# Gated mix of linear attention and PEER: the sum of the key features taken as one product of ones with a prepared tile

## The chip, the cores and the metric

The kernel runs on one core of a Trainium2 chip. The metric is the device time of one execution in microseconds, from start to end. PE stands for the matrix engine, PEld for its weight loads, DVE, ACT and POOL for the vector, scalar and GpSimd engines, SP for the engine that only issues DMAs.

## The reference

The input x has 2048 rows of 512 values. Two branches read it and a gate mixes them. Branch B is a PEER layer with 32 heads and one expert per head: scores of two halves of a query, the best of 16 in each, a row of u and v chosen by the pair. Branch A is linear attention with 32 heads of 16 and softmax features:

```python
phi_q = concat([softmax(pq), softmax(-pq)]); phi_k = concat([softmax(pk), softmax(-pk)])
kv = einsum("bhsf,bhsd->bhfd", phi_k, v)
z  = einsum("bhsf->bhf", phi_k)          # the sum over all 2048 rows
num = einsum("bhqf,bhfd->bhqd", phi_q, kv)
den = einsum("bhqf,bhf->bhq", phi_q, z)[..., None] + 1e-6
return g * (num / den) @ wo + (1 - g) * b
```

The change concerns z: 32 heads times 32 features, 1024 sums over all rows. Since every row of x needs all of kv and z, the key features of all rows come ahead of the first use of either.

## The kernel before

The rows are worked in 16 tiles of 128, numbered 0 to 15. Single-precision products are split in two parts, a high one and the rest (names ending in h and l, type fp32r), and one logical product is three matmuls: lines L56, L57 and L58 of a helper. The order of every engine's instructions is the order of the Python text; nothing reorders it. An engine takes its list in order, and waits where an operand or a buffer isn't ready.

Stage A (until about 127 us) makes for each tile the key logits `pk`, the features `phis[t]` (tile `d`, 128 rows by 1024: ACT's exponential, then in `ksoft` a DVE sum L200, a DVE reciprocal L201, and POOL's product L202 that normalises), and the values `vs[t]` with a 17th column of ones per head. `kvacc(t)` (L209) is 32 small products, two records each, that add phi_k^T v into one PSUM bank `acc`; the 17th column of that bank collects z, but only for tiles 0 to 13, since the values of tiles 14 and 15 are made later, without the column. For those two, `kvz(t)` (L217) multiplies the features by a column `ones` into the same 17th column, 32 products again. At the end of stage A `fold_q` (L148) folds the feature weights into the query weights, in two halves of PE work; between and after these stand the scores `s` of tile 0 (`front_s(0, 0)`, `front_s(0, 1)`). ACT (wah, L153) and DVE (wal, L154) then split the folded weights.

Between the stages, after `kvz(14)`, come for tile 0: `best` (DVE L475 and L476: maximum and mask of a score), the transposing DMA of that mask to `et` (SP, L482), `front_q` (PE: `pq`), `soft_in` (DVE L94, L96, L98, L100: differences to maximum and minimum, into a new tile `d`), `front_p` (PE: `pp`), then `kvz(15)`. ACT copies z out of the bank into `zc` (128 partitions by 8), `z_final` spreads it over all partitions with eight products of a broadcast column of zc and the identity, in plain fp32 (L663), and ACT copies the outcome to `zb` (128 by 1024, L665).

Stage B goes over the tiles a = 0 to 14 in a loop, and each pass also begins tile a + 1. DVE's gate reciprocal (L390) releases ACT's L398, L399 and L400 (`gelu_act`), behind which stand on ACT's list the two exponentials L426 (`soft_exp`). DVE sums them (L436), POOL multiplies them with zb (L432, `soft_w`), and DVE goes on to the denominators and to `best` and `soft_in` of the next tile. On PE a pass holds `mk` (the mask's product with `et`), `s` of the next tile in two halves, `pp` and `pq`. In pass 1 alone the values of tiles 14 and 15 are made (`pv`, ACT copy L189) and `kvacc(14)` and `kvacc(15)` close the bank, which ACT copies out in `kv_final` (`kvb`, L657). On ACT's list those four copies stand behind L586, which waits for POOL's `cf` (L581); on POOL's list L581 stands behind L432, L755 and L404. PE's `oT` (L518) is the first to use kvb. The bank pools of PSUM have four buffers (`mm`) and three (`tr`).

Of the kernel before, what the change touches and what calls it, by code (L numbers as in the profile page):

```python
# [9 lines left out]
F32 = mybir.dt.float32  # L10
F32R = mybir.dt.float32r
# [5 lines left out]
ALU = mybir.AluOpType  # L17
# [3 lines left out]
P = 128  # L21
# [5 lines left out]
F = 16  # L27
# [8 lines left out]
def mix_kernel(ctx, tc, xT, wqT, wkT, wv, wphi, wo, wq, kk, ug, ev, cst, out):  # L36
# [6 lines left out]
    def mm_bank(name):  # L43
        return psum.tile([P, 512], F32, tag="mm", bufs=4, name=name)
# [32 lines left out]
    kp = per.tile([P, 2, 2, 32], F32, name="kp")  # L77
    sa.append(per.tile([P, 4, 24], U16, name="sa1"))
    sb = [per.tile([P, 4, 24], U16, name=f"sb{i}") for i in range(2)]
    ones = per.tile([P, 1], F32, name="ones")  # L80
    zc = per.tile([P, 8], F32, name="zc")
    per.tile([P, 96], F32, name="rest")

# [56 lines left out]
    def fold_q(raw, wh, wl):  # L140
        o = four("foldq")
        for i in range(2):
            for k in (2 * i, 2 * i + 1):
                for b in range(NK):
                    for q in range(4):
                        r = slice(32 * q, 32 * q + 32)
                        c0 = (k * NK + b) * 32
                        pe.matmul(o[q][:, c0:c0 + 32], raw[r, b, k * P:(k + 1) * P], wp[r, b, :],  # L148
                                  start=True, stop=True, skip_group_check=True)
            yield  # L150
        for q in range(4):
            part = o[q].rearrange("p (g c) -> p g c", c=32)
            act.copy(fv(wh, q), part)  # L153
            dve.tensor_tensor(fv(wl, q), part, fv(wh, q), op=ALU.subtract)  # L154
        yield
# [42 lines left out]
    def ksoft(t):  # L198
        d, st = phis[t], stk.pop(t)
        dve.tensor_reduce(st[:, 64:128], g64(d), axis=AX.X, op=ALU.add)  # L200
        dve.reciprocal(st[:, 128:192], st[:, 64:128])  # L201
        pool.tensor_tensor(g64(d), g64(d), b64(st[:, 128:192]), op=ALU.mult)  # L202

    def kvacc(t):
        n = F + 1 if t < NT - 2 else F
        for g in range(8):
            for c in range(4):
                h = 4 * g + c
                pe.matmul(acc[32 * c:32 * c + 32, g, :n], phis[t][:, 32 * h:32 * h + 32],  # L209
                          vs[t][:, h, :n], start=(t == 0 and g == 0),  # L210
                          stop=(t == NT - 1), skip_group_check=True)

    def kvz(t):
        for g in range(8):
            for c in range(4):
                h = 4 * g + c
                pe.matmul(acc[32 * c:32 * c + 32, g, F:], phis[t][:, 32 * h:32 * h + 32],  # L217
                          ones, start=False, stop=False, skip_group_check=True)

    def score_w(i, raw):  # L220
        j, par = i // 2, i % 2
        if par == 0:
# [48 lines left out]
    for a in sa + sb:  # L271
        pool.memset(a, 0)
    pool.memset(kvb, 0.0)
    pool.memset(ones, 1.0)
    for k in (0, 2, 1, 3):
        if k == 0:
            x_split(0, slice(0, 1))
# [26 lines left out]
    for t in range(NT):  # L304
        if t + 3 < NT:
            x_load(t + 3)
        if 2 < t < NT - 2:
            vproj(t)()
        kproj(t)
        old = [] if t == NT - 3 else list(joins)  # L310
        if old:
            joins.clear()
        for _ in range(plan.get(t, 0)):
            score_w(done, raws[done])
            done += 1
            if done + 1 < 16:
                raws.append(stage(wq[done + 1], f"wq{done + 1}"))
            elif done == 15:
                rawq = stage(wqT, "rawq")
            if done % 2 == 0:  # L320
                score_planes(done // 2 - 1)
        if t == 11:
            rawu = [spare(ug[:, 0:2], "rawu0", [P, 2, NU])]
        if t == 12:
            rawu.append(spare(ug[:, 2:4], "rawu1", [P, 2, NU]))
        if t == 13:
            rawe = [spare(ev[:, 0], "rawe0", [P, D])]
        if t % 2 == 0:
            for u in (t - 3, t - 2):
                if u >= 0:  # L330
                    kvacc(u)
        if 0 < t < NT - 2:
            x_split(t + 2)
        if t == NT - 2:
            score_join(*old.pop())
        elif t == NT - 1:
            for k in range(2):
                split(eh[:, k, :], el[:, k, :], rawe[k])
            fq = fold_q(rawq, wah, wal)
            next(fq)  # L340
            front_s(0, 0)
            next(fq)
            front_s(0, 1)
            kvacc(NT - 3)
            next(fq)
        act.activation(phis[t], phis[t], AF.Exp)  # L346
        if t == NT - 2:
            score_join(*joins.pop())
        if t == 13:
            for k in range(NK):  # L350
                split(uh[:, k, :NU], ul[:, k, :NU], rawu[k // 2][:, k % 2, :])
            rawe.append(spare(ev[:, 1], "rawe1", [P, D]))
        ksoft(t)
        for j, tp in old:
            score_join(j, tp)
    ca.close()
    w2 = ctx.enter_context(tc_pool("w2", "left"))
    zb = w2.tile([P, 1024], F32, name="zb", bufs=1)
    chains = {}

    def step(t, n=1):
# [44 lines left out]
    def front_q(t):  # L406
        pq = mm_bank(f"pq{t}")
        proj(pq, t, wah, wal, 0, D)
        st8[t]["pq"] = pq
# [246 lines left out]
            r = slice(32 * c, 32 * c + 32)  # L656
            act.copy(kvb[r, :, F * (c % 2):F * (c % 2) + F], acc[r, :, :F])  # L657

    def z_final():
        for j in range(2):  # L660
            o = mm_bank(f"z{j}")
            for g in range(4):
                pe.matmul(o[:, g * P:(g + 1) * P], zc[:, 4 * j + g:4 * j + g + 1].to_broadcast([P, P]), ident,  # L663
                          start=True, stop=True)
            act.copy(zb[:, 512 * j:512 * j + 512], o)  # L665

    def wo_load(ks):
        for k in ks:
# [1 line left out]
            sp.dma_start(rawo[k], wo[:, k, :])  # L670

    rawo = {}
    kvz(NT - 2)
    best(0, 0)
    best(0, 1)
    cb.close()
    w3 = ctx.enter_context(tc_pool("w3", "left"))
    turn_eq(0)
    front_q(0)
    soft_in(0)  # L680
    front_p(0, False)
    kvz(NT - 1)
    act.copy(zc, acc[:, :, F])
    gelu_pre(0)
    z_final()
    wo_load((0, 1))
    def dealt(a, b, z):
        def first():
            for _ in gate(a):
                step(b)  # L690
            step(b, 4)
            if z >= 0:
                back_cl(z)

        moves = iter((first, lambda: step(b, 5), lambda: step(b, 2), lambda: None))
        return lambda: next(moves)()

    for a in range(NT - 1):
        n, b, z = a + 1, a - 1, a - 2
        owed = min(18, 3 * max(0, a - DEFER))  # L700
        left = min(18, 3 * max(0, a - DEFER + 1))
        B, Z = b >= 0, z >= 0
        if Z:
            mid_num(z)
        if B:
            planes(b, 0)
            if Z:
                c_join(z)
            planes(b, 1)
            front_q(a)  # L710
        if owed:
            back(z - 1, owed)
            store(z - 1)
        if a == 1:
            v14, v15 = vproj(NT - 2), vproj(NT - 1)
        gelu_in(a)
        if Z:
            num_lo(z)
        if B:
            soft_in(a, dealt(a, b, z))  # L720
            drain(b)
        else:
            for _ in gate(a):
                pass
        gelu_act(a)
        if a == 1:
            v14()
        soft_exp(a)
        if a == 1:
            v15()  # L730
            for k in range(2):
                act.copy(wbh[:, k, :], rawo[k])
        if Z and not left:
            back(z)
            store(z)
        if not left:
            mid_mask(a)
        front_s(n, 0)
        if left:
            mid_mask(a)  # L740
            if left < 18:
                back(z, 18 - left)
        if a == 1:
            kvacc(NT - 2)
            kvacc(NT - 1)
            cl_.close()
            w4 = ctx.enter_context(tc_pool("w4", "right"))
        front_s(n, 1)
        front_p(n, False)
        soft_w(a)  # L750
        soft_sum(a, 0)
        soft_sum(a, 1)
        if a == 1:
            for k in range(2):
                pool.tensor_tensor(wbl[:, k, :], rawo[k], wbh[:, k, :], op=ALU.subtract)  # L755
            wo_load((2, 3))
        best(n, 0)
        soft_y(a, 0)
        soft_y(a, 1)
        soft_p(a)  # L760
        if B:
            join(b)
            gelu_out(b)
            coef(b)
            c_planes(b)
        if a == 1:
            kv_final()
            for k in range(2, NK):
                act.copy(wbh[:, k, :], rawo[k])
        soft_b(a)  # L770
        if a == 1:
            for k in range(2, NK):
                pool.tensor_tensor(wbl[:, k, :], rawo[k], wbh[:, k, :], op=ALU.subtract)
        best(n, 1)
        turn_eq(n)
        gelu_pre(n)
    a, b, z = NT - 1, NT - 2, NT - 3
    neg = w2.tile([P, P], F32R, name="neg", bufs=1)

    def low(lo, o, hi):  # L780
        pe.matmul(o, neg, hi, start=False, stop=True, skip_group_check=True)
# [118 lines left out]
```

## Time and profile before

| what | value |
|---|---|
| time, three runs | 379.95, 380.48 and 380.8 us, median 380.48 us |
| span of the profiled execution (first to last instruction) | 378.1 us |
| that execution's clock | PE granted full speed in all 40 slices |
| PE busy | 372.5 us, 99% of the span |
| DVE, ACT, POOL busy | 315.9, 235.5 and 154.9 us |
| DMA | 46.69 MB, mean 123 GB/s |

The profiled execution has its span of 378.1 us as its own time; the runs were timed from start to end of the program, so that 2.4 us of a median run lie outside of the span. A row of the timeline begins with its start and its duration in us; an instruction's record overlaps with that of the next one on the same engine, so that the price of one in a row of equals is the distance from start to start. "x64" says that neighbouring instructions of one form are joined in a row. In brackets stands how long the engine had nothing to do before, and what ended that.

### The profile page before, as it was taken

Reading aid. Unit: us, or ns where it says so; the run is one execution under the profiler, and the core shown is the slowest. Engines: PE = TensorE matmul, PEld = TensorE weight load, DVE = VectorE, ACT = ScalarE, POOL = GpSimd, SP = SyncE. Lnnn points to the kernel's source line nnn. Section 1 sums busy time; section 2 is a strip of 40 time slices with the busy share of each in tenths; the row PEclk is TensorE's granted clock in tenths of the full one; section 3 lists DMA queues with packets and bytes.
Section 4 is the critical chain, followed back from the end, with each engine's and each line's share of the span. In section 5 each row is a group of like instructions: output and inputs, shape, how many; then the busy total and the mean of one; then the engine's idle time right before and its main releaser. Section 6 shows DMA issues by size and latency. Waiting matters only on the chain.

```text
span 378.1 us, 9073 instructions
## 1 busy us (share of the span) xinstructions
PE 372.5 (99%) x3613; PEld 294.3 (78%) x3613; DVE 315.9 (84%) x776; ACT 235.5 (62%) x420; POOL 154.9 (41%) x164
## 2 busy tenths in 40 slices
PE   8999999999999999999999999999999999999996
PEld 4766777777768888888878888888888888888775
DVE  4479866866868968879999999999999999999993
ACT  4436554644646345769668777696686686687741
POOL 1014435325325232946427335344454454364700
PEclk9999999999999999999999999999999999999999
DMA  7757878478592034242351452441532524523201
GB/s 272 307 187 259 258 218 237 157 222 237 188 305 84 3 85 83 73 83 76 80 99 49 105 84 57 85 100 32 121 62 65 127 56 72 126 52 77 64 34 57
DMA packets 72219, 46.69 MB, mean 123 GB/s; under 512 B 63600, under 2 KB 64496, under 8 KB 69872
## 3 DMA queue, kind: packets, MB, share of 16 engines
q1 hardware_dynamic: 71312, 45.24, 44.6%
q10 hardware_dynamic: 864, 0.87, 0.8%
q8 instruction: 28, 0.46, 0.5%
q14 instruction: 15, 0.12, 0.1%
HBM read 26.43 MB, written 4.19 MB: 81 GB/s over the span
## 4 chain that ended last, share of the span: by engine, by line
PE 97%; DMA 1%; ACT 0%; SPq 0%; DVE 0%; issue 0%; ACTq 0%; DVEq 0%
PE po L627 11%; PE s L56 8%; PE s L57 8%; PE s L58 8%; PE po L634 5%; PE pq L56 5%; PE pv L56 4%; PE pk L56 4%; PE ws L225 4%; PE pv L57 4%; PE pq L58 4%; PE pk L57 4%; PE pq L57 4%; PE pk L58 4%; PE pv L58 4%; PE oT L518 3%
## 5 line engine op out<-in xcount | busy, mean ns | idle before, releaser
L432 POOL TENSOR_TENSOR w<-d,zb 128x512 f32<-128x512 f32 x32 | 40.9, 1294 | 83.4 <-ACT d L426 81.1
L202 POOL TENSOR_TENSOR d<-d,st 128x1024 f32<-128x1024 f32 x16 | 31.0, 1935 | 74.4 <-DVE st L201 40.5
L56 PE MATMUL s<-sh,xh 128*128 128x512 f32 x128 | 51.0, 399 | 0.0
L57 PE MATMUL s<-sl,xh 128*128 128x512 f32 x128 | 49.9, 390 | 0.0
L58 PE MATMUL s<-sh,xl 128*128 128x512 f32 x128 | 49.8, 389 | 0.0
L426 ACT ACTIVATE d<-d 128x512 f32<-128x512 f32 x32 | 20.1, 632 | 38.0 <-DVE d L98 29.3
L467 POOL TENSOR_TENSOR d<-d,st 128x512 f32<-128x512 f32 x30 | 31.2, 1062 | 28.5 <-DVE st L461 25.6
L509 ACT COPY pt<-tp 128x1024 uint16<-128x1024 uint16 x28 | 36.4, 1369 | 1.0 <-PE kvacc L209 1.0
L346 ACT ACTIVATE d<-d 128x1024 f32<-128x1024 f32 x16 | 17.0, 1064 | 28.5 <-DVE d L100 28.5
L499 ACT COPY pl<-d 128x1024 uint16<-128x1024 uint16 x28 | 29.2, 1045 | 4.4 <-POOL d L467 4.4
L58 PEld LDWEIGHTS s<-sh,xl 128*128 128x128 f32 x128 | 24.0, 188 | 5.1
L56 PEld LDWEIGHTS s<-sh,xh 128*128 128x128 f32 x128 | 24.0, 188 | 4.7
L57 PEld LDWEIGHTS s<-sl,xh 128*128 128x128 f32 x128 | 24.1, 188 | 4.5
L56 PE MATMUL pq<-wah,xh 128*128 128x512 f32 x64 | 26.7, 418 | 0.0
L56 PE MATMUL pv<-wbh,xh 128*128 128x512 f32 x64 | 26.0, 407 | 0.0
L436 DVE TENSOR_REDUCE st<-d 128x32 f32<-128x512 f32 x32 | 21.7, 683 | 5.0 <-ACT d L426 3.5
L57 PE MATMUL pv<-wbl,xh 128*128 128x512 f32 x64 | 25.2, 394 | 0.3 <-DVE wbl L51 0.3
L200 DVE TENSOR_REDUCE st<-d 128x64 f32<-128x1024 f32 x16 | 19.5, 1218 | 7.0 <-ACT d L346 7.0
L56 PE MATMUL pk<-wah,xh 128*128 128x512 f32 x64 | 25.3, 396 | 0.0
L58 PE MATMUL pv<-wbh,xl 128*128 128x512 f32 x64 | 25.1, 392 | 0.0
L58 PE MATMUL pq<-wah,xl 128*128 128x512 f32 x64 | 25.1, 392 | 0.0
L57 PE MATMUL pk<-wal,xh 128*128 128x512 f32 x64 | 25.0, 391 | 0.0
(177 smaller groups left out, 1029.5 us busy)
## 6 DMA issues: line engine op xcount, KB each, us to landing
wq<-wq SPq DMA_DIRECT2D x16, 1024.0 KB, 6.0
xr<-xT SPq DMA_DIRECT2D x15, 256.0 KB, 6.0
y<-ot SPq DMA_DIRECT2D x15, 256.0 KB, 2.3
rawk<-wkT SPq DMA_DIRECT2D x1, 1024.0 KB, 6.1
rawq<-wqT SPq DMA_DIRECT2D x1, 1024.0 KB, 5.7
rawo<-wo SPq DMA_DIRECT2D x4, 256.0 KB, 3.8
rawu<-ug SPq DMA_DIRECT2D x2, 258.0 KB, 6.3
rawv<-wv ACTq DMA_DIRECT2D x2, 256.0 KB, 4.2
```

The costliest lines, as they stand in the source:

```text
L56: pe.matmul(o, ah, bh, start=(first and i == 0), stop=False)
L57: pe.matmul(o, ah, bl, start=False, stop=False)
L58: pe.matmul(o, al, bh, start=False, stop=(last and i == n - 1))
L200: dve.tensor_reduce(st[:, 64:128], g64(d), axis=AX.X, op=ALU.add)
L202: pool.tensor_tensor(g64(d), g64(d), b64(st[:, 128:192]), op=ALU.mult)
L426: act.activation(hs(d, i), hs(d, i), AF.Exp)
L432: pool.tensor_tensor(hs(e["w"], i), hs(e["ph"], i), hs(zb, i), op=ALU.mult)
L436: dve.tensor_reduce(pair(e["st"][:, 64:128])[:, :, i], hs(e["ph"], i), axis=AX.X, op=ALU.add)
L467: eng.tensor_tensor(g64(d)[:, gs_], g64(d)[:, gs_], r[:, gs_].unsqueeze(2).to_broadcast([P, 32, F]), op=ALU.mult)
L499: act.copy(pl, e["ph"][:, halves[i]].bitcast(U16).rearrange("p (c j) -> p j c", j=2))
L509: act.copy(p16[:, :, 4 * i:4 * i + 4, :], e["tp"][i].rearrange("p (j g) n -> p j g n", j=2))
L627: pe.matmul(po, a, b, start=(i == 0), stop=False)
```

## The change

z is no longer gathered in the bank to its end. The 17th column is read after tile 13, which therefore has to come first: `kvacc(13)` moves on PE from behind the scores of tile 0 to the place between the first half of `fold_q` and those scores, and ACT's copy to `zc` from behind `kvz(15)` to ahead of the four casts L153. A tile `zsum` (128 by 1024) is made: POOL writes the identity times zc, 128 columns for each of 8 groups (the diagonal), and adds the features of tile 14; both stand on POOL's list ahead of the normalising product of tile 15, behind a memset that fills `neg` with ones (a tile that is filled anew with minus the identity at the program's end, as before). DVE adds the features of tile 15 in two halves, ACT casts each half to its high part, DVE makes the rest. Four matmuls of fp32r, ones by the high part and ones by the rest for each half, sum over the partitions and leave z in every partition. Both `kvz` and the eight fp32 products go. `front_s(1, 0)`, the first half of the next tile's scores, moves ahead of these four matmuls and of `mk`.

The list of SP is unchanged: each transposing DMA and each load stands where it stood. The diff, cut to its core:

```diff
-    def kvz(t):
-        for g in range(8):
-            for c in range(4):
-                h = 4 * g + c
-                pe.matmul(acc[32 * c:32 * c + 32, g, F:], phis[t][:, 32 * h:32 * h + 32],
-                          ones, start=False, stop=False, skip_group_check=True)
...
         elif t == NT - 1:
+            fq = fold_q(rawq, wah, wal)
+            next(fq)
+            kvacc(NT - 3)
             for k in range(2):
                 split(eh[:, k, :], el[:, k, :], rawe[k])
-            fq = fold_q(rawq, wah, wal)
-            next(fq)
+            act.copy(zc, acc[:, :, F])
             front_s(0, 0)
             next(fq)
             front_s(0, 1)
-            kvacc(NT - 3)
             next(fq)
...
-        ksoft(t)
+        if t < NT - 1:
+            ksoft(t)
...
+    neg = w2.tile([P, P], F32R, name="neg", bufs=1)
+    pool.memset(neg.bitcast(F32), 1.0)
+    zsum = w2.tile([P, 1024], F32, tag="w", bufs=1, name="zsum")
+    pool.tensor_tensor(zsum.rearrange("p (g n) -> p g n", n=P), ident.unsqueeze(1).to_broadcast([P, 8, P]),
+                       zc.unsqueeze(2).to_broadcast([P, 8, P]), op=ALU.mult)
+    pool.tensor_tensor(zsum, zsum, phis[NT - 2], op=ALU.add)
+    ksoft(NT - 1)
...
-    def z_final():
-        for j in range(2):
-            o = mm_bank(f"z{j}")
-            for g in range(4):
-                pe.matmul(o[:, g * P:(g + 1) * P], zc[:, 4 * j + g:4 * j + g + 1].to_broadcast([P, P]), ident,
-                          start=True, stop=True)
-            act.copy(zb[:, 512 * j:512 * j + 512], o)
+    def z_parts(z):
+        out = []
+        for i, s_ in enumerate(halves):
+            zh = w3.tile([P, 512], F32R, tag="pl", name=f"zh{i}")
+            zl = w3.tile([P, 512], F32R, tag="tp", name=f"zl{i}")
+            dve.tensor_tensor(z[:, s_], z[:, s_], phis[NT - 1][:, s_], op=ALU.add)
+            act.copy(zh, z[:, s_])
+            out.append((zh, zl))
+        for (zh, zl), s_ in zip(out, halves):
+            dve.tensor_tensor(zl, z[:, s_], zh, op=ALU.subtract)
+        return out
+
+    def z_final(parts):
+        for (zh, zl), s_ in zip(parts, halves):
+            o = tr_bank("z")
+            pe.matmul(o, neg, zh, start=True, stop=False)
+            pe.matmul(o, neg, zl, start=False, stop=True)
+            act.copy(zb[:, s_], o)
...
-    kvz(NT - 2)
     best(0, 0)
     best(0, 1)
...
     front_q(0)
+    zparts = z_parts(zsum)
     soft_in(0)
     front_p(0, False)
-    kvz(NT - 1)
-    act.copy(zc, acc[:, :, F])
     gelu_pre(0)
-    z_final()
+    front_s(1, 0)
+    z_final(zparts)
     wo_load((0, 1))
...
-        front_s(n, 0)
+        if a:
+            front_s(n, 0)
```

Three places of the engines' lists show it. The new text has other line numbers: behind the new lines all of stage B stands one line later up to 644 or so (L94 stays, L475 becomes L476, L432 becomes L433). First PE, from the end of tile 0's `pp` to the first of `mk`, before:

```order
L58 MATMUL pp_1667<-uh,xl 128x258
L217 MATMUL kvacc<-ones,d_1450 32x1 x32
L663 MATMUL z_1721<-cs,zc 128x128 x4
L663 MATMUL z_1727<-cs,zc 128x128 x4
L537 LDWEIGHTS et_1646
```

and after, from the last of the twelve matmuls of `s` of tile 1, first half, which follow `pp`:

```order
L58 MATMUL s_1_1671<-sh,xl 128x512
L675 MATMUL z<-zh_1634,neg 128x512
L676 MATMUL z<-zl_1635,neg 128x512
L675 MATMUL z<-zh_1638,neg 128x512
L676 MATMUL z<-zl_1639,neg 128x512
L538 LDWEIGHTS et_1619
```

The two kinds of plain fp32 products are gone, four matmuls of fp32r stand there, and the scores of tile 1 stand ahead of them. Second DVE, from the mask of tile 0's second half to the sums of pass 0, before:

```order
L476 TENSOR_TENSOR eq_1635<-s_0_1541,mx_0_1639 128x512
L94 TENSOR_REDUCE st_1662<-pq_1648 128x32
L96 TENSOR_REDUCE st_1662<-pq_1648 128x32
L98 TENSOR_TENSOR d_1661<-pq_1648,st_1662 128x32x16
L100 TENSOR_TENSOR d_1661<-st_1662,pq_1648 128x32x16
L390 RECIPROCAL gs_1713<-gs_1713 128x1
L436 TENSOR_REDUCE st_1662<-d_1661 128x32 x2
```

and after:

```order
L477 TENSOR_TENSOR eq_1608<-s_0_1573,mx_0_1612 128x512
L665 TENSOR_TENSOR zsum<-zsum,d_1449 128x512 x2
L669 TENSOR_TENSOR zl_1635<-zsum,zh_1634 128x512
L669 TENSOR_TENSOR zl_1639<-zsum,zh_1638 128x512
L94 TENSOR_REDUCE st_1645<-pq_1621 128x32
L96 TENSOR_REDUCE st_1645<-pq_1621 128x32
L98 TENSOR_TENSOR d_1644<-pq_1621,st_1645 128x32x16
L100 TENSOR_TENSOR d_1644<-st_1645,pq_1621 128x32x16
L391 RECIPROCAL gs_1663<-gs_1663 128x1
L437 TENSOR_REDUCE st_1645<-d_1644 128x32 x2
```

Four instructions of 128 by 512 stand ahead of all of `soft_in`, and so of the reciprocal for which ACT waits. Third POOL, from the normalising product of tile 14 to pass 0's product with zb, before:

```order
L202 TENSOR_TENSOR d_1347<-d_1347,st_1348 128x1024
L202 TENSOR_TENSOR d_1450<-d_1450,st_1451 128x1024
L394 TENSOR_TENSOR x_1717<-x_1717,px_1716 128x256
L432 TENSOR_TENSOR w_1792<-d_1661,zb 128x32x16 x2
L467 TENSOR_TENSOR d_1661<-d_1661,st_1662 128x512 x2
```

and after:

```order
L202 TENSOR_TENSOR d_1346<-d_1346,st_1347 128x1024
L354 MEMSET neg 128x128
L356 TENSOR_TENSOR zsum<-cs,zc 128x1024
L358 TENSOR_TENSOR zsum<-zsum,d_1346 128x1024
L202 TENSOR_TENSOR d_1449<-d_1449,st_1450 128x1024
L395 TENSOR_TENSOR x_1667<-x_1667,px_1666 128x256
L433 TENSOR_TENSOR w_1738<-d_1644,zb 128x32x16 x2
```

Three instructions stand between the normalising products of tiles 14 and 15. By the program's semaphores the memset waits for DVE's first `el` (L51, whose input lay in the same memory), and the product L356 for ACT's zc and for the last matmul of `fold_q`.

More of the change, by code (lines that the diff above doesn't have):

```diff
@@ L79, in mix_kernel @@
     sb = [per.tile([P, 4, 24], U16, name=f"sb{i}") for i in range(2)]
-    ones = per.tile([P, 1], F32, name="ones")
+    per.tile([P, 1], F32, name="ones")
     zc = per.tile([P, 8], F32, name="zc")
@@ L273, in mix_kernel @@
     pool.memset(kvb, 0.0)
-    pool.memset(ones, 1.0)
     for k in (0, 2, 1, 3):
@@ L777, in mix_kernel @@
     a, b, z = NT - 1, NT - 2, NT - 3
-    neg = w2.tile([P, P], F32R, name="neg", bufs=1)
     def low(lo, o, hi):
```

## The prediction

> **What bounds the kernel now.** I read the page's busy shares and chain first, then the busy time by stretches, then the timeline of each engine from 118 to 161 us, where all changed instructions lie but for two short ones at the start.
>
> ```profile
> PE 372.5 (99%) x3613; PEld 294.3 (78%) x3613; DVE 315.9 (84%) x776; ACT 235.5 (62%) x420; POOL 154.9 (41%) x164
> ...
> PE 97%; DMA 1%; ACT 0%; SPq 0%; DVE 0%; issue 0%; ACTq 0%; DVEq 0%
> ```
>
> PE is the bound of the whole, and the chain of waits runs on it to 97%. So PE time that goes is gained, as long as no other engine then arrives later than PE. The stretches (us, then busy time and count for PE, PEld, DVE, ACT and POOL, granted clock) say how near the others are around the change:
>
> ```profile
> 130.00:135.00 5.00, 4.72 (x96) 4.36 (x95) 3.94 (x8) 1.94 (x7) 1.55 (x2) 1.00 0.35 64
> 135.00:145.00 10.00, 10.00 (x59) 8.56 (x59) 6.64 (x19) 4.96 (x12) 4.82 (x6) 1.00 0.17 49
> 145.00:160.00 15.00, 15.00 (x229) 12.13 (x227) 13.74 (x37) 10.19 (x20) 8.60 (x10) 1.00 0.39 95
> ```
>
> Only at 130 to 135 does PE idle at all, 0.28 us. DVE has some 3.4 us to spare at 135 to 145 and hardly any, 1.3 us, at 145 to 160. What DVE gets to do there decides.
>
> **PE: what goes and what comes.** PE's timeline:
>
> ```profile
> 126.52 0.71 PE L209 MATMUL kvacc<-v,d 128*32 128x17 f32 x62
> ...
> 127.09 0.71 PE L217 MATMUL kvacc<-ones,d 128*32 128x1 f32 x62
> 127.74 0.50 PE L56 MATMUL pq<-wah,xh 128*128 128x512 f32 x1
> ...
> 132.16 0.71 PE L217 MATMUL kvacc<-ones,d 128*32 128x1 f32 x64
> 133.15 2.05 PE L663 MATMUL z<-cs,zc 128*128 128x128 f32 x16 [0.28 <-ACT zc L683]
> 135.04 0.35 PE L537 MATMUL mk<-wm,et 128*128 128x16 bf16 x8
> ...
> 135.79 0.39 PE L58 MATMUL s<-sh,xl 128*128 128x512 f32 x1
> ...
> 140.56 0.39 PE L58 MATMUL s<-sh,xl 128*128 128x512 f32 x1
> ...
> 153.54 1.27 PE L209 MATMUL kvacc<-v,d 128*32 128x16 f32 x128
> 154.74 0.50 PE L56 MATMUL s<-sh,xh 128*128 128x512 f32 x1
> ```
>
> - `kvacc(13)` and `kvz(14)` take 127.74 - 126.52 = 1.22 us together, 0.61 each. `kvz(14)` goes: -0.61. `kvacc(13)` only moves; what stands between its new place and its old one comes 0.61 later, the second half of `fold_q` among it.
> - `kvz(15)`, the wait for zc and the eight fp32 products go: from 132.16 to 135.04, -2.88.
> - A 512-column matmul of fp32r costs (140.56 - 135.79) / 21 = 0.227 us. Four come: +0.91. `front_s(1, 0)` costs the same wherever it stands.
>
> PE's own sum is -0.61 - 2.88 + 0.91 = -2.6 us. If that were all, the time would be 377.9 us.
>
> **DVE and ACT: what comes and who waits.** DVE's timeline, then ACT's:
>
> ```profile
> 122.53 2.28 DVE L51 TENSOR_TENSOR el<-rawe,eh 128x512 fp32r<-128x512 f32 x2
> 124.73 2.47 DVE L154 TENSOR_TENSOR wal<-foldq,wah 128x512 fp32r<-128x512 f32 x4
> ...
> 130.82 0.69 DVE L476 TENSOR_TENSOR eq<-s,mx 128x512 bf16<-128x512 f32 x1
> 131.43 0.68 DVE L94 TENSOR_REDUCE st<-pq 128x32 f32<-128x512 f32 x1
> ...
> 133.82 0.16 DVE L390 RECIPROCAL gs<-gs 128x1 f32<-128x1 f32 x1
> ...
> 137.42 1.28 DVE L436 TENSOR_REDUCE st<-d 128x32 f32<-128x512 f32 x2 [3.45 <-ACT d L426]
> ...
> 143.44 0.69 DVE L476 TENSOR_TENSOR eq<-s,mx 128x512 bf16<-128x512 f32 x1
> 145.18 0.69 DVE L94 TENSOR_REDUCE st<-pq 128x32 f32<-128x512 f32 x1 [1.05 <-PE pq L58]
> ...
> 149.75 0.68 DVE L98 TENSOR_TENSOR d<-pq,st 128x512 f32<-128x512 f32 x1
> ```
>
> ```profile
> 123.67 2.06 ACT L153 CAST wah<-foldq 128x512 fp32r<-128x512 f32 x4 [2.22 <-PE foldq L148]
> ...
> 132.94 0.17 ACT L683 COPY zc<-kvacc 128x8 f32<-128x8 f32 x1 [6.26 <-PE kvacc L217]
> ...
> 135.72 0.20 ACT L398 ACTIVATE gs<-gs 128x1 f32<-128x1 f32 x1
> ...
> 136.77 1.14 ACT L426 ACTIVATE d<-d 128x512 f32<-128x512 f32 x2
> ...
> 150.47 0.63 ACT L426 ACTIVATE d<-d 128x512 f32<-128x512 f32 x1 [1.99 <-DVE d L98]
> ...
> 152.26 0.57 ACT L189 COPY v<-pv 128x512 f32<-128x512 f32 x1
> ...
> 157.81 0.62 ACT L586 COPY plc<-cf 128x512 uint16<-128x512 uint16 x1 [0.34 <-POOL cf L581]
> 158.34 1.07 ACT L657 COPY kvb<-kvacc 32x128 f32<-32x128 f32 x4
> ```
>
> - ACT's casts wah wait for `fold_q` and so start at 123.67 + 0.61 with the copy zc (at most 0.17) ahead of them: 124.4. One takes 2.06 / 4 = 0.5, so DVE's first wal can start at 125.0 in place of 124.73. DVE's list is 0.3 late from there on.
> - Four new DVE instructions, two SBUF inputs of 128 by 512 each. Their nearest rows are wal, 2.47 / 4 = 0.62, and the undisturbed el, 0.68 (row below): 2.5 to 2.7, I take 2.58. They start at 131.73. The two casts to zh (0.5 like wah) lie beside the second add and the first subtraction, and ACT has nothing else then (6.26 us idle ahead of 132.94). So `soft_in(0)` starts at 131.43 + 0.3 + 2.58 = 134.31.
> - L390 follows 133.82 - 131.43 = 2.39 later, at 136.70, ending at 136.86. ACT's L398, at 135.72 before, waits for it: +1.15. ACT's copies of zb, which held L398 up before, start behind z at about 134.9 and are over by 136.1; that wait covers them. Behind L398 stand both L426, for which DVE's L436 waits: 138.57. Of DVE's 3.45 us of waiting, 1.75 are left.
> - From L436 to the mask of tile 1's second half DVE hardly stops, so that mask ends at 143.44 + 0.69 + 1.15 = 145.28. Before, DVE then waited 1.05 us for PE's `pq`, until 145.18. Now `pq` has long been there, and L94 of tile 1 starts at 145.28: **+0.1 against before**. 2.88 us of delay have used up 1.70 + 1.05 of waiting.
>
> From there the chain no longer passes PE. The rows of POOL and of the weight loads of `oT`:
>
> ```profile
> 1.58 0.32 POOL L273 MEMSET kvb<- 128x256 f32 x1
> ...
> 121.73 1.93 POOL L202 TENSOR_TENSOR d<-d,st 128x1024 f32<-128x1024 f32 x1
> 129.09 1.94 POOL L202 TENSOR_TENSOR d<-d,st 128x1024 f32<-128x1024 f32 x1 [5.43 <-DVE st L201]
> ...
> 151.18 2.55 POOL L432 TENSOR_TENSOR w<-d,zb 128x512 f32<-128x512 f32 x2 [5.48 <-ACT d L426]
> 153.69 2.56 POOL L755 TENSOR_TENSOR wbl<-rawo,wbh 128x512 fp32r<-128x512 f32 x2
> ...
> 157.04 0.74 POOL L581 TENSOR_TENSOR cf<-cf,px 128x256 f32<-128x256 f32 x1
> ```
>
> ```profile
> 159.46 0.40 PEld L518 LDWEIGHTS oT<-pt,kvb 64*32 64x32 f32 x30 [0.16 <-ACT kvb L657]
> ```
>
> L98 of tile 1 releases L426 (150.47), that releases POOL's L432 (151.18), behind it without a pause come L755 and L581, that releases ACT's L586 (157.81), behind it stand the kvb copies, and PE's `oT` waits for them already, 0.16 us. All of it moves by +0.1. PE arrives with its lead, loses a part at `kvacc(15)` (the copy of v, from 152.26, ends at 152.93; the next `s` starts 0.6 later, at 153.5 against 154.74, a lead of 1.2) and the rest at `oT`. After that, PE-bound as before.
>
> **POOL.** The memset: 128 by 128, under 0.32. The diagonal product has broadcast inputs, like L202: 1.93; with two full inputs, like L755, it would be 2.56. The addition has two full inputs: 2.56. Start at about 124.5 (the end of `fold_q`, 0.61 later than 123.67; and zc). The pair ends at 129.0 to 129.6, where L202 of tile 15 started at 129.09 before, now 129.4 by DVE's 0.3. L202 then ends at 131.3 to 131.6, before DVE's first addition, at 131.73: cost nothing, with 0.1 to 0.4 us left of cover. The two memsets, `ones` gone and `neg` come, lie at no edge. SP's issues keep their order; the transposed mask is due 0.3 later, and `mk` comes after z.
>
> **The sum.** Span 378.1 + 0.1 = 378.2. The median run lay 2.4 us above the span: 380.6 us. Bounds of this case: DVE's four at 2.5 with no shift of wal, -0.3; at 2.7 with POOL 0.2 late, +0.3. That is 380.2 to 381.0.
>
> **Rivals.**
>
> *Faster: DVE's delay is absorbed.* DVE waits 3.45 + 1.05 = 4.5 us between 133.8 and 145.2, more than the 2.88 that come. If L436 weren't tied to L390 through ACT's list, L94 of tile 1 could start 1.05 earlier, the kvb chain would follow, and the time would be 379.4 us. Against it: L398 stands ahead of L426, and its operand comes from L390. The full 377.9 needs kvb off the path as well, against the 0.16 us that `oT` waits already. 0.12 and 0.08.
>
> *Slower: POOL's pair makes tile 15's features late.* DVE's first addition waits for L202 of tile 15, and all above hangs on it 1 to 1. The point is a pair of 5.0 us: 124.5 + 5.0 = 129.5, with 1.94 and a handover 131.5 to 131.7. Each microsecond more costs one. The diagonal product, with both inputs broadcast and in stretches of 128, has no row of its own; at 1 us above its upper bound, 3.6, the time is 381.7 us. Against: POOL's rows go by size, and broadcasting made them shorter, not longer. 0.14.
>
> *Slower: DVE and POOL collide.* The view by line of L51 (count, then shortest, median and longest in ns):
>
> ```profile
> L51 DVE TENSOR_TENSOR el<-rawe,eh x2: 680/1180/1681, 122.5 to 124.1; 128x512 fp32r<-128x512 f32 x2
> ```
>
> The first el took 1.68 us, under POOL's L202 (121.73 to 123.66), the second 0.68. If POOL's diagonal product gets ahead of the second el, that one waits up to 1.93 to 2.56 us, wal, both masks and all of `soft_in` with it: 380.6 + 2 = 382.6 us. The point: the product would have to start before the second el, at 124.1. Against: it waits for `fold_q`, 124.3, and stands behind a memset that waits for the first el. 0.09.
>
> The Trainium skill, page "SBUF — State Buffer", section "Who interferes with whom", states that a DVE instruction with two SBUF inputs and a GpSimd instruction that reads SBUF exclude each other, whoever comes first for its whole length. The two el agree with it, 1.68 against 0.68. By this rule the order at 124.1 to 124.3 decides between this rival and the forecast, 382.6 or 380.6 us; and the four new DVE instructions, of the same kind, cost 0.62 only while POOL stands still, as it does between L202 of tile 15 and the next pass.
>
> **How the numbers follow.** No change (what a measurement of this kernel can tell is about 0.2%, 0.76 us): 0.54, with rounding the rest of 0.57 split to both sides. Faster 0.12 + 0.08 and a bit, 0.21; slower 0.14 + 0.09 and a bit, 0.25. The range leaves out the full gain (0.08) and the collision (0.09): 379.3 to 382.0. The likeliest case alone spans 380.2 to 381.0.
>
> **What would show it.** Right: `mk` of tile 0 about where it was, but `s` of tile 1's second half over 2 us earlier; DVE's wait before L436 down to 1.5 to 2 us and the one before `soft_in(1)` gone; PE waiting some 1.4 us at `kvacc(15)` for v and some 1 us at `oT` for kvb; the kvb copies at 158.4. Wrong: L94 of tile 1 before 144.6 or after 146.0; `oT` not waiting; POOL's pair over 5.0 us; the second el over 0.7.

## The result, and the profile after

The changed kernel takes 380.82 us (median of 14 runs, 380.68 to 381.18), the kernel before in the same comparison 380.53 us. The ratio is 1.0006 with a 95% interval of 0.9997 to 1.0016, from 0.1 us faster to 0.6 us slower: no difference that can be told. The forecast was 380.6 us, between 379.3 and 382.0, no change as the likeliest.

PE's saving is in the profile. Its busy time on the page went from 372.5 to 370.8 us, in a span of 379.0 us. From the page of the changed kernel, the busy shares and the chain that ended last:

```profile
PE 370.8 (98%) x3473; PEld 292.3 (77%) x3473; DVE 319.8 (84%) x780; ACT 236.2 (62%) x422; POOL 159.0 (42%) x166
...
PE 87%; DVE 6%; DMA 1%; ACT 1%; POOL 1%; issue 1%; SPq 0%; ACTq 0%; DVEq 0%
```

The chain ran on PE to 97% before. Now 8% of it runs on DVE, ACT and POOL. PE's three longest waits (line, releaser, us in total, times, longest):

```profile
PE kvacc L209 <- ACT v L189: 1.7, 1, 1.7
PE warm L263 <- POOL tab L246: 1.2, 1, 1.2
PE oT L519 <- ACT kvb L658: 0.8, 1, 0.8
```

The wait at `warm` was there before. The two others are new, 2.42 us together, nearly all of what PE had saved. PE's timeline:

```profile
117.03 1.99 PE L148 MATMUL foldq<-wp,rawq 32*128 32x32 f32 x64
118.94 0.74 PE L209 MATMUL kvacc<-v,d 128*32 128x17 f32 x64
...
134.57 0.40 PE L675 MATMUL z<-zh,neg 128*128 128x512 f32 x1
...
135.51 0.36 PE L538 MATMUL mk<-wm,et 128*128 128x16 bf16 x8
135.72 0.47 PE L56 MATMUL s<-sh,xh 128*128 128x512 f32 x1
...
153.86 0.73 PE L209 MATMUL kvacc<-v,d 128*32 128x16 f32 x64 [1.66 <-ACT v L189]
...
159.76 1.21 PE L519 MATMUL oT<-pt,kvb 64*32 64x128 f32 x32 [0.76 <-ACT kvb L658]
```

The same places before the change, `fold_q`, the second half of tile 1's scores and `oT`:

```profile
116.80 1.99 PE L148 MATMUL foldq<-wp,rawq 32*128 32x32 f32 x64
...
138.06 0.39 PE L56 MATMUL s<-sh,xh 128*128 128x512 f32 x1
...
159.16 0.96 PE L518 MATMUL oT<-pt,kvb 64*32 64x128 f32 x32
```

The second half of tile 1's scores starts at 135.72, against 138.06 before: the lead is there. It is spent at 153.86 and 159.76, and inside of `oT`, which takes 1.21 us in place of 0.96 because its later parts wait for the later copies of kvb. DVE in between:

```profile
131.95 1.28 DVE L665 TENSOR_TENSOR zsum<-zsum,d 128x512 f32<-128x512 f32 x2
133.31 1.30 DVE L669 TENSOR_TENSOR zl<-zsum,zh 128x512 fp32r<-128x512 f32 x2
134.53 0.68 DVE L94 TENSOR_REDUCE st<-pq 128x32 f32<-128x512 f32 x1
...
138.81 1.28 DVE L437 TENSOR_REDUCE st<-d 128x32 f32<-128x512 f32 x2 [1.74 <-ACT d L427]
...
145.44 0.68 DVE L94 TENSOR_REDUCE st<-pq 128x32 f32<-128x512 f32 x1
146.04 0.15 DVE L391 RECIPROCAL gs<-gs 128x1 f32<-128x1 f32 x1
146.11 0.28 DVE L554 TENSOR_TENSOR m<-sa 128x64 uint16<-128x64 uint16 x1
146.31 0.72 DVE L556 TENSOR_TENSOR m<-sa 128x32 uint16<-128x32 uint16 x1
147.07 0.42 DVE L564 TENSOR_TENSOR X<-m,m 128x256 uint32<-128x256 uint32 x1
...
150.64 0.68 DVE L98 TENSOR_TENSOR d<-pq,st 128x512 f32<-128x512 f32 x1
```

The four new instructions take 134.53 - 131.95 = 2.58 us, and the 3.45 us of waiting before the sums of pass 0 shrank to 1.74. ACT's rows show the tie: the copies of zb are over at 136.31, and then L399 waits for DVE's reciprocal.

```profile
135.24 1.07 ACT L677 COPY zb<-z 128x512 f32<-128x512 f32 x2
137.11 0.20 ACT L399 ACTIVATE gs<-gs 128x1 f32<-128x1 f32 x1 [0.80 <-DVE gs L391]
```

Up to L94 of tile 1 all stands as worked out. Then one small instruction, L556, takes 0.72 us, where the same (L555) took 0.17 before. POOL's timeline says what stood there:

```profile
124.85 2.09 POOL L356 TENSOR_TENSOR zsum<-cs,zc 128x1024 f32<-128x1024 f32 x1
127.02 2.41 POOL L358 TENSOR_TENSOR zsum<-zsum,d 128x1024 f32<-128x1024 f32 x1
129.58 1.94 POOL L202 TENSOR_TENSOR d<-d,st 128x1024 f32<-128x1024 f32 x1 [0.16 <-DVE st L201]
...
144.23 2.08 POOL L468 TENSOR_TENSOR d<-d,st 128x512 f32<-128x512 f32 x2 [2.78 <-issue]
146.26 0.74 POOL L395 TENSOR_TENSOR x<-x,px 128x256 f32<-128x256 f32 x1
```

POOL's product x of tile 1 runs from 146.26 to 147.00, and L556 ends then, at 147.03. Before, the same product was over at 145.70, ahead of both mask instructions, as the rows of POOL and DVE before show:

```profile
144.96 0.74 POOL L394 TENSOR_TENSOR x<-x,px 128x256 f32<-128x256 f32 x1
```

```profile
145.98 0.17 DVE L555 TENSOR_TENSOR m<-sa 128x32 uint16<-128x32 uint16 x1
```

In the eleven traces of this document the first half of `fold_q` starts between 116.80 and 117.55 us, and ahead of it the change takes out one memset and nothing else. So traces are compared below by the time since the first half of `fold_q` starts (117.03 here, 116.80 before). Its distance to the end of the span is 379.0 - 117.03 = 261.97 us here and 261.30 before: +0.67 us in these two executions. Spans are given to a tenth, so such a distance is good to 0.05 us and a difference of two to 0.1.

### The profile page after: what moved, and what is told of

The parts are those of the page before. It is cut to its first block, busy times and chain, and to the rows that moved or that the text cites. A ratio compares the mean times of both kernels' runs of the same rounds, so it can differ in the third digit from the quotient of the medians.

```text
span 379.0 us, 8798 instructions
## 1 busy us (share of the span) xinstructions
PE 370.8 (98%) x3473; PEld 292.3 (77%) x3473; DVE 319.8 (84%) x780; ACT 236.2 (62%) x422; POOL 159.0 (42%) x166
## 4 chain that ended last, share of the span: by engine, by line
PE 87%; DVE 6%; DMA 1%; ACT 1%; POOL 1%; issue 1%; SPq 0%; ACTq 0%; DVEq 0%
PE po L628 11%; PE s L56 7%; PE s L58 6%; PE s L57 6%; PE po L635 5%; PE pq L56 4%; PE pk L56 4%; PE ws L218 4%; PE pk L57 4%; PE pk L58 4%; PE pv L56 4%; PE pq L58 3%; PE pv L57 3%; PE pq L57 3%; PE pv L58 3%; PE oT L519 3%
## 5 line engine op out<-in xcount | busy, mean ns | idle before, releaser
L433 POOL TENSOR_TENSOR w<-d,zb 128x512 f32<-128x512 f32 x32 | 40.9, 1294 | 83.8 <-ACT d L427 80.9
L202 POOL TENSOR_TENSOR d<-d,st 128x1024 f32<-128x1024 f32 x16 | 31.0, 1937 | 69.7 <-DVE st L201 36.0
L468 POOL TENSOR_TENSOR d<-d,st 128x512 f32<-128x512 f32 x30 | 31.2, 1061 | 28.4 <-DVE st L462 25.6
L57 PE MATMUL pq<-wal,xh 128*128 128x512 f32 x64 | 25.1, 392 | 0.0
```

What stands on the lines that cost most here:

```text
L57: pe.matmul(o, ah, bl, start=False, stop=False)
L433: pool.tensor_tensor(hs(e["w"], i), hs(e["ph"], i), hs(zb, i), op=ALU.mult)
L468: eng.tensor_tensor(g64(d)[:, gs_], g64(d)[:, gs_], r[:, gs_].unsqueeze(2).to_broadcast([P, 32, F]), op=ALU.mult)
```

## The experiments

In the table, "L98" is the start of that DVE instruction for tile 1 (the differences for which ACT's exponentials wait), "kvb" the start of the first copy, and "end" the end of the span, each since `fold_q` of the same trace. Ratios are against the kernel before, run on the same chip.

| kernel | median us | ratio (95%) | L98 | kvb | end |
|---|---|---|---|---|---|
| before | 380.53 | | 32.95 | 41.54 | 261.30 |
| changed | 380.82 | 1.0006 (0.9997 to 1.0016) | 33.61 | 42.16 | 261.97 |
| e1 before, no z on PE | 378.40 | 0.9944 (0.9931 to 0.9957) | 30.88 | 39.45 | 259.22 |
| e2 gate first | 380.25 | 0.9991 (0.9983 to 1.0) | 32.70 | 41.27 | 261.04 |
| e3 x of tile 1 early | 380.41 | 0.9998 (0.999 to 1.0007) | 33.01 | 41.59 | 261.35 |
| e4 no z on DVE | 380.22 | 0.9991 (0.9982 to 1.0) | 32.69 | 41.26 | 261.07 |
| e5 both e2 and e3 | 380.00 | 0.9986 (0.9977 to 0.9994) | 32.61 | 41.16 | 261.00 |
| e6 v and kvb ahead | 380.66 | 0.9997 (0.9988 to 1.0006) | 33.62 | 39.61 | 261.44 |
| e7 before, v and kvb ahead | 380.75 | 1.0005 (0.9996 to 1.0014) | 32.93 | 40.52 | 261.47 |
| e8 all four moves | 379.59 | 0.9970 (0.9958 to 0.9982) | 32.61 | 38.61 | 260.44 |
| e9 e8 and xh ahead | 379.27 | 0.9969 (0.9959 to 0.9979) | 32.64 | 38.64 | 260.49 |

In the first six rows and in e5 the three last columns move together: from L98 to kvb it is 8.55 to 8.59 us, from L98 to the end 228.34 to 228.39. What L98 loses or gains, the end loses or gains, as long as the copies of v and kvb stand where they stood.

Behind pass 2's `mk` nothing more is won or lost. That `mk` starts 50.20 us after `fold_q` in the kernel before, 50.81 in the changed one and 49.27 in e8; the last `oT` starts at 249.23, 249.85 and 248.35. The differences, +0.6 and -0.9, stay the same over these 200 us. So all that follows is about the 50 us between the start of `fold_q` and that `mk`.

### e1: PE's work taken away and nothing put in its place

```diff
     def z_final():
         for j in range(2):
-            o = mm_bank(f"z{j}")
-            for g in range(4):
-                pe.matmul(o[:, g * P:(g + 1) * P], zc[:, 4 * j + g:4 * j + g + 1].to_broadcast([P, P]), ident,
-                          start=True, stop=True)
-            act.copy(zb[:, 512 * j:512 * j + 512], o)
+            act.copy(zb[:, 512 * j:512 * j + 512], phis[NT - 1][:, 512 * j:512 * j + 512])
...
-    kvz(NT - 2)
...
-    kvz(NT - 1)
     act.copy(zc, acc[:, :, F])
     gelu_pre(0)
+    front_s(1, 0)
     z_final()
...
-        front_s(n, 0)
+        if a:
+            front_s(n, 0)
```

> The kernel before without any of PE's z work: both kvz and the eight fp32 products left out (zb is then a copy of the features of tile 15, and the output's attention is wrong by that), scores of tile 1 moved ahead as in the change, nothing added on DVE or POOL. PE is 0.61 + 2.88 = 3.5 us shorter. Theory (the chain DVE, ACT, POOL, kvb decides): DVE loses its 1.05 us of waiting before the differences of tile 1 and nothing more, so oT comes 1.1 us earlier: 379.4 us, with PE waiting over 2 us at kvacc(15) and oT together. Rival (PE alone decides): 380.5 - 3.5 = 377.0 us.

Measured 378.4 us, between the two. The rows of e1 that tell why, ACT and DVE:

```profile
133.53 1.12 ACT L661 COPY zb<-d 128x512 f32<-128x512 f32 x2
134.56 0.20 ACT L398 ACTIVATE gs<-gs 128x1 f32<-128x1 f32 x1
```

```profile
136.25 1.28 DVE L436 TENSOR_REDUCE st<-d 128x32 f32<-128x512 f32 x2 [1.82 <-ACT d L426]
...
142.88 0.68 DVE L94 TENSOR_REDUCE st<-pq 128x32 f32<-128x512 f32 x1
...
143.54 0.38 DVE L553 TENSOR_TENSOR m<-sa 128x64 uint16<-128x64 uint16 x1
143.84 0.72 DVE L555 TENSOR_TENSOR m<-sa 128x32 uint16<-128x32 uint16 x1
```

Without z on PE the zb copies wait for no matmul, so ACT's L398 behind them comes earlier too, and DVE's sums with it: 136.25 - 117.28 = 18.97 since `fold_q`, against 20.62 before. The expectation had overlooked that. L94 gains 2.78 (25.60 against 28.38), the two mask instructions stand beside POOL's and give 0.17 and 0.55 back, and L98, kvb and end gain 2.07, 2.09 and 2.08. So the chain decides, not PE's 3.5 us, though its gain was 2.1 and not 1.1. The forecast of over 2 us of waiting on PE missed with it: PE waits 0.5 us at `oT`, 0.3 at `mk` of tile 0, and not at `kvacc(15)`. The run also gives an estimate of the most that the change's idea can bring with everything else as it stands, the collision among it: about 2.1 us, and that with z at no cost to anybody.

### e2 and e4: DVE's part

e2 moves one instruction:

```diff
     zparts = z_parts(zsum)
-    soft_in(0)
     front_p(0, False)
     gelu_pre(0)
+    for _ in gate(0):
+        pass
+    soft_in(0)
     front_s(1, 0)
...
             drain(b)
-        else:
-            for _ in gate(a):
-                pass
         gelu_act(a)
```

> The changed kernel with one DVE instruction moved: the gate's reciprocal ahead of the differences of tile 0 in place of behind them. Theory: DVE's delay passes on through ACT's list, so the reciprocal at about 134.6 in place of 136.9 lets ACT go on when the zb copies end (136.3), DVE's sums of pass 0 start at 137.9 in place of 138.8, and the differences of tile 1, kvb and oT come 0.9 us earlier: 379.9 us. Rival (the kvb chain is bound by something of its own in pass 1): no change, 380.8 us.

e4 leaves the four DVE instructions out:

```diff
             zh = w3.tile([P, 512], F32R, tag="pl", name=f"zh{i}")
-            zl = w3.tile([P, 512], F32R, tag="tp", name=f"zl{i}")
-            dve.tensor_tensor(z[:, s_], z[:, s_], phis[NT - 1][:, s_], op=ALU.add)
             act.copy(zh, z[:, s_])
-            out.append((zh, zl))
-        for (zh, zl), s_ in zip(out, halves):
-            dve.tensor_tensor(zl, z[:, s_], zh, op=ALU.subtract)
+            out.append((zh, zh))
         return out
```

> The changed kernel without the four DVE instructions: the features of tile 15 and the low part are left out of z (the four matmuls use the high part twice, z is wrong by that). Theory: DVE's differences of tile 0 start at about 132.0 in place of 134.5, but the reciprocal is then no longer what ACT waits for; the zb copies are, and they end at about 136.2 as before, so the gain is that of the moved reciprocal and not 2.6 us: 379.9 us. Rival (DVE's 2.6 us count in full as soon as they go): 378.2 us. Rival (kvb bound in pass 1): 380.8 us.

Both came out alike, 380.25 and 380.22 us, and in the traces 0.93 and 0.90 us earlier at the end than the changed kernel. In the runs it is 0.6 us by medians, though the changed kernel was not run beside them; every run of e2 lies below every run of the changed kernel (at most 380.52 against at least 380.68 us), while e4 has one of 380.89. The rows of DVE and of ACT's copies of zb, e2 first:

```profile
134.73 0.16 DVE L391 RECIPROCAL gs<-gs 128x1 f32<-128x1 f32 x1
...
138.13 1.28 DVE L437 TENSOR_REDUCE st<-d 128x32 f32<-128x512 f32 x2 [0.86 <-ACT d L427]
```

```profile
135.45 1.07 ACT L677 COPY zb<-z 128x512 f32<-128x512 f32 x2
```

and e4:

```profile
134.21 0.15 DVE L391 RECIPROCAL gs<-gs 128x1 f32<-128x1 f32 x1
137.80 1.28 DVE L437 TENSOR_REDUCE st<-d 128x32 f32<-128x512 f32 x2 [3.44 <-ACT d L427]
```

```profile
135.12 1.07 ACT L673 COPY zb<-z 128x512 f32<-128x512 f32 x2 [1.80 <-PE z L672]
```

Since `fold_q` the sums start at 20.87 in both. Taking away all 2.58 us of DVE's work bought no more than moving a 0.16 us reciprocal, since in both runs the reciprocal is early enough and ACT's copies of zb, which start 18.19 us after `fold_q` in both, are what ACT's L399 has to wait for. The rivals (378.2; 380.8) fall. This settles the first rival of the prediction: DVE had the room, and the tie through ACT's list was what made its delay count. Both runs have the collision of the next section, with 0.73 us for L556.

### e3 and e5: the collision

```diff
-        gelu_in(a)
+        if a != 1:
+            gelu_in(a)
...
+        if a == 0:
+            gelu_pre(n)
+            gelu_in(n)
         soft_b(a)
...
         turn_eq(n)
-        gelu_pre(n)
+        if a:
+            gelu_pre(n)
```

> The changed kernel with one POOL instruction moved: the product x of tile 1 ahead of the two normalising products of tile 0, where POOL waits anyway, in place of behind them. Theory (DVE's second mask instruction m took 0.72 us in place of 0.17 because it had to wait for that POOL product): m takes under 0.3 us, the maxima and minima behind it come 0.55 us earlier, kvb and oT too: 380.3 us. Rival (the 0.9 us of the profiled spans are a late start and nothing else): m stays or its delay is taken up again, 380.8 us.

POOL and DVE in e3:

```profile
142.20 0.74 POOL L395 TENSOR_TENSOR x<-x,px 128x256 f32<-128x256 f32 x1 [0.26 <-ACT x L386]
```

```profile
146.80 0.17 DVE L556 TENSOR_TENSOR m<-sa 128x32 uint16<-128x32 uint16 x1
```

With the POOL product elsewhere, L556 takes 0.17 again, L98 comes 0.60 earlier than in the changed kernel and the end 0.62: 261.35, within 0.05 of before (261.30). So nearly all of the profiled difference of 0.67 us between the two kernels is this collision. The runs, 380.41 us with a ratio of 0.9998 to before, agree with it and could not show it alone.

e5 has both moves, e2's and e3's.

> The changed kernel with both single moves: the gate's reciprocal ahead of the differences of tile 0, and POOL's product x of tile 1 ahead of the normalising products of tile 0. In the traces the minima-side differences of tile 1 (DVE L98) came 0.9 us earlier by the one and 0.6 by the other, counted from the start of the first half of fold_q. Theory (one chain through that instruction, so the two add): 1.5 us earlier than in the changed kernel, kvb and the end too: 379.5 us or a little less. Rival (the two shorten the same wait, or another limit comes first): no more than 0.9 us, 380.0 us.

They do not add: 380.00 us, the rival's value, with the end at 261.00 against 261.04 of e2. The rows of e5, POOL and DVE:

```profile
142.07 0.74 POOL L395 TENSOR_TENSOR x<-x,px 128x256 f32<-128x256 f32 x1 [1.15 <-ACT x L386]
```

```profile
142.23 0.66 DVE L455 TENSOR_TENSOR st<-st 128x64 f32<-128x64 f32 x1
...
146.24 0.17 DVE L556 TENSOR_TENSOR m<-sa 128x32 uint16<-128x32 uint16 x1
```

The product now meets another small DVE instruction, L455, which takes 0.22 us in e2 and 0.66 here. 0.55 us were won and 0.44 lost again. The theory of one chain stands; the sum failed by a second collision that the expectation had not priced. Against the kernel before, e5 is the first of these kernels that works out z in full and is faster clear of the noise, by 0.5 us (ratio 0.9986, 0.9977 to 0.9994).

### e6 and e7: the two waits of PE

```diff
         if a == 1:
             v14()
+            v15()
         soft_exp(a)
         if a == 1:
-            v15()
             for k in range(2):
...
             coef(b)
+            if a == 1:
+                kv_final()
             c_planes(b)
         if a == 1:
-            kv_final()
             for k in range(2, NK):
```

> The changed kernel with two moves on ACT's list in pass 1: the copy of v of tile 15 ahead of the exponentials of tile 1 (it then needs only PE's pv), and the four kvb copies ahead of the plane copy that waits for POOL's cf. Nothing upstream is changed. Theory (PE's lead of 2.5 us is there and is lost at v and kvb alone): kvacc(15) no longer waits, kvb is ready at 157.8 in place of 159.7, oT starts there, and 1.5 to 2 us of PE's lead last to the end: 379.2 us. Rival (DVE is late by then and PE waits for it in pass 2 instead): 380.6 us.

> The kernel before with the same two moves on ACT's list in pass 1. PE has no lead there: it waits for v not at all and for kvb 0.16 us. Theory: 0.1 to 0.2 us faster than before at most, 380.3 us, so that what e6 wins is the change's own PE time. Rival (the kvb order itself holds the kernel up, change or no change): as much as in e6, 378.9 us.

In e6 PE no longer waits for v or kvb; `oT` starts at 157.24, 2.55 us earlier since `fold_q` than in the changed kernel. But the end moves by 0.53 only, and the runs show 380.66 us, the rival's time. What PE waits for from 118 to 165 us in e6:

```profile
PE po L628 <- ACT xh L523: 1.2, 1, 1.2
```

```profile
158.72 0.62 ACT L587 COPY plc<-cf 128x512 uint16<-128x512 uint16 x1 [0.99 <-POOL cf L582]
...
162.24 0.63 ACT L523 CAST xh<-oT 128x256 fp32r<-128x256 f32 x2
```

ACT's copies xh of the outcome of `oT` stand behind the plane copy that waits for POOL's cf, behind two casts and the five reads of `pp`. They start 45.18 us after `fold_q`, against 45.72 in the changed kernel: 0.54 earlier, as the end is. The plane copy has not moved (41.66 against 41.63), since cf still hangs on the chain of L98. The lead passed two waits and met the next. The rival had said that DVE would be late; it was ACT's list first, and behind 165 us DVE's rest of the coefficients for 0.2 us more. On the kernel before (e7) the same moves win nothing, 380.75 us, so they are worth something only where PE has a lead.

### e8 and e9: all of it, and a kernel that is faster

e8 is the changed kernel with the edits of e2, e3 and e6.

> The changed kernel with all four moves: gate, x of tile 1, v and kvb. Theory: kvb comes at about 156 and PE reaches oT at its own pace, 2.6 us earlier than before; DVE, 1.5 us earlier than in the changed kernel, is then ready for tile 2 before PE: 378.0 us, the whole of PE's 2.6 us. Rival (DVE becomes the bound in the passes after): 379.0 us, with DVE's wait for pq of tile 2 gone.

Measured 379.59 us, ratio 0.9970 (0.9958 to 0.9982): faster than before by 0.9 us, less than the theory (2.5) and the rival (1.5) had. PE reaches `oT` 2.41 us earlier than before since `fold_q` (39.95 against 42.36), and then waits 0.96 us at `po` for xh. e9 moves xh ahead of the five reads of `pp` of tile 2:

```diff
         if Z:
             mid_num(z)
+        if a == 2:
+            gelu_pre(a)
         if B:
...
         turn_eq(n)
-        if a:
+        if a > 1:
             gelu_pre(n)
```

> The kernel of e8 with one more move on ACT's list: the two copies of oT (xh, L523), for which PE's first po waited 0.96 us in e8, ahead of the five reads of pp of tile 2 (1.3 us). Theory (the rest of PE's lead is lost at this wait): po follows pq without a wait, 0.9 us earlier, and that lasts to the end: 378.7 us. Rival (DVE is the bound by then, since its differences of tile 3 waited for no pq in e8): 379.4 us or more, with po's wait gone but a wait of PE in pass 2 or 3 in its place.

That wait is gone, and the end is where it was (260.49 against 260.44); 379.27 us, with a ratio of 0.9969 against 0.9970 in e8. PE's waits from 118 to 175 us in e9:

```profile
PE po L628 <- POOL wbl L792: 0.5, 1, 0.5
PE po L635 <- DVE cl L619: 0.3, 1, 0.3
```

POOL's rest of the output weights and DVE's rest of the coefficients take the place of ACT's copy. The rival had forecast another wait in its place and at least 379.4 us; the wait is there, on POOL and DVE each in part, and 379.27 is nearer to it than to the theory's 378.7. Both e8 and e9 are faster than before, and by their medians than the changed kernel, which was not run beside them; some 0.9 to 1.1 of PE's 2.6 us are then gained. The rest is lost between `po` and `mk` of pass 2, where PE arrives 2.5 us early in e9 and leaves 0.8 us early. What it would need was not tried.

## Why the prediction was right

- *PE's sum, -2.6 us.* Right. Since `fold_q`, the second half of tile 1's scores starts at 135.72 - 117.03 = 18.69 against 138.06 - 116.80 = 21.26: -2.57. The waits that took it back are at the two forecast places, 1.66 us at `kvacc(15)` (1.4 forecast) and 0.76 at `oT` (1).
- *wal 0.3 late.* Right: 125.21 - 117.03 = 8.18 in the changed kernel against 124.73 - 116.80 = 7.93, 0.25. The cover of the zh casts held.
- *DVE's four at 2.58 us.* Right, 2.58. L437 waits 1.74 us, 1.75 had been worked out. L94 of tile 1 starts at 28.41 against 28.38, +0.03 for a forecast of +0.1.
- *The step from L94 on, "all of it moves by +0.1".* Here a term was missing, the one step of the forecast mechanism that failed. L98, kvb and end moved by 0.66, 0.62 and 0.67; the kvb copies, one of the signs named for being right, came 0.56 later than forecast. Since `fold_q`, DVE's sums of pass 0 came 1.16 us later. DVE itself took nearly all of that up in the 1.05 us for which it had waited for `pq`, but POOL's product x of tile 1 moved by the delay (28.16 to 29.23), and so onto a small DVE instruction that had moved by 0.10. e3 showed it by taking that product away. The time stayed inside the likeliest case's own range all the same (380.2 to 381.0), and that was luck in part: nothing in the prediction kept such a meeting at 0.55 us, or at one.
- *From span to time, 2.4 us.* Misread, in the part ahead of the prediction too. In every run whose span is on record the time lies 1.7 to 1.9 us above it. So some 1.8 us of a run lie outside of the span, and the other 0.6 only say that the profiled execution of the kernel before was faster than the median. The forecast of 380.6 isn't hurt: it comes to the median plus 0.1 us. But the difference of the two profiled spans, 0.9 us, is no measure of the change.
- *The bounds.* -0.3 and +0.3 around 380.6 give 380.3 to 380.9; the prediction wrote 380.2 to 381.0. The measured 380.82 lies in both.
- *POOL costs nothing.* Right, and closer than it reads: POOL's addition and DVE's reciprocal L201, the two that L202 of tile 15 needs, both ended at 129.43. L202 then ended at 131.52, 0.43 us ahead of DVE's first addition. The diagonal product took 2.09 us (1.93 to 2.56 were given), the addition 2.41 (2.56), the memset 0.21. The point of the rival in which this pair decides was not reached: the two took 4.58 us, from 124.85 to 129.43, against 5.0.
- *The rival of absorbed delay, 379.4 us.* Its condition was right and did not hold in the changed kernel; e2 made it hold, and L94 of tile 1 then started 27.49 us after `fold_q`, 0.89 earlier than before, where 1.05 had been worked out. At the end 0.26 of it was left (261.04 against 261.30), since e2 has the collision too.
- *The rival of the collision.* Right about the mechanism, wrong about the place and so about the price. At the second el it did not happen: the diagonal product started at 124.85, behind the second el's start at 124.5, and that one took 0.68 us as before (the shortest in the row of L51 below, in ns; the longest is the first el, beside L202 as before). It happened 21 us later, for 0.55 and not 2 us. The Trainium skill, page "SBUF — State Buffer", section "Who interferes with whom", says that DVE and GpSimd share a port pair as an exclusive lock, and that issue order and not the shape of an instruction decides who blocks; the traces agree, since L556 ended with POOL's product, and L554, which started 0.2 us before the end of POOL's L468, took 0.28 us in place of 0.21: what was lost depended on when an instruction started and not on its own length. The row that would have shown how widely this counts stood in the trace of before: the same L454 as in e5 took 0.64 us there in pass 1, beside POOL's L404 (156.22 to 156.96), and 0.22 in pass 0.

```profile
L51 DVE TENSOR_TENSOR el<-rawe,eh x2: 679/1232/1786, 122.8 to 124.5; 128x512 fp32r<-128x512 f32 x2
```

```profile
141.36 0.22 DVE L454 TENSOR_TENSOR st<-st 128x64 f32<-128x64 f32 x1
...
156.40 0.64 DVE L454 TENSOR_TENSOR st<-st 128x64 f32<-128x64 f32 x1
```

## What to carry to other kernels

A saving on the bounding engine is worth what the next chain leaves of it: follow the new work through the list of every engine that it delays, to the point where the saved engine waits again, and price the change there. To leave out DVE's 2.58 us of work here won no more than to move a 0.16 us reciprocal ahead of the work behind it, so order counted before amount. And where an instruction on POOL moves in time, look up which DVE instructions with two SBUF inputs it now overlaps, the smallest too.

## What the runs showed of the hardware

A DVE instruction of 128 by 32 that takes 0.17 us alone took 0.72 us beside a POOL product of 0.74 us, and one of 128 by 64 took 0.66 in place of 0.22; on the chain each such meeting cost 0.44 to 0.55 us, and the first of them is nearly the whole difference of the two profiled executions since `fold_q`. An in-place POOL addition of 128 by 1024 took 2.41 us, less than two of 128 by 512 with full inputs (2.56); a product of two broadcast inputs took 1.99 to 2.09, near the 1.93 of one with a single broadcast input.
